# Attention and a hyper-mixer on one core: the third batch's load ahead of the output weights, later loads half a batch earlier, and x transposed in two 64-row tiles

## Chip, cores, metric

One core of a Trainium2 chip. The metric is the device time of one execution in microseconds (us). Each kernel was run several times beside the kernel before on the same chip. A profiled execution is one of them; times inside it count from its first instruction. TensorE's clock is given as a share of full speed; a "dip" is a stretch at half of it. A run is marked slow when it is over 1.5% above the fastest of the same kernel; ratios leave slow runs out.

## The reference

Eight batches. Each is grouped-query attention (16 query heads, 4 key/value heads, 384 rows, head size 64), whose output x [384, 1024] goes through a mixer and an output product:

```python
scores = scale * q @ k.T ; attn = softmax(scores) ; x = attn @ v      # per head, heads joined
wq, wk = x @ w_q, x @ w_k                                              # [384, 64] each
mixed  = (scale * wq @ wk.T) @ x
out    = relu(mixed) @ w_out                                           # [384, 1024]
```

## The kernel before

Batches are numbered from 0. One batch has 18 "scores" (pairs of matmuls, L259, for two heads in two 64-row tiles of TensorE), each followed by one exponential on ScalarE. Every three scores end in an attention step that writes a part of x (`xnat`). Two such steps complete one 128-row block of x. The first two blocks of batches 1 to 7 are transposed by DMA, the third by TensorE; then the product of x with w_q and w_k (`wqk`) reads all three. A small scheduler in the program fixes TensorE's order when the kernel is built, using guessed times such as `DMA_TR` for a DMA transpose. If a guess is wrong, TensorE waits in that order.

```python
def load(b):                       # keys, queries in two halves, values; 2.36 MB; all on the SP queue
    ...
def tr_dma(b, part):               # part 0: keys; parts 1 to 3: queries of one 128-row block
    ...
    nc.sync.dma_start_transpose(out=KT, ...)              # or QT[...]
    ready["K", b, kp] = clk["pe"] + DMA_TR                # the scheduler's guess
def attend(b, g, u):
    ...                            # attention of one group; when a block of x is whole:
    if x_by_dma(b, c) and kp == KP - 1:
        x_tr_dma(b, c)             # nc.sync.dma_start_transpose(out=xTs[b][:, :, c, :], ...)
def x_by_dma(b, c):
    return b > 0 and c < C - 1
def x_tr(b, c):                    # by TensorE: eight 128x128 transposes into one PSUM bank, one copy
    ...
def after_s(b, s):                 # after score s of batch b
    n = b + 1
    if b == 0 or n >= B: return
    if s == 0: load(n)
    elif s == 5: cast(n); start_tr(n)
    elif s in (9, 11, 13, 15): tr_dma(n, (s - 9) // 2)
# the start, cut
load(0); ...; load(1)
# w_q, w_k: two loads; then the output weights, 4.19 MB in four pieces:
for dc in range(0, DC, 2):
    nc.sync.dma_start(out=wld[:, dc:dc + 2, :], in_=moe_w_out[...])
```

Keys and queries of batches 0 and 1 are transposed by TensorE, those of later batches by DMA. Each of these DMA instructions goes to one in-order queue on SP; loads, DMA transposes and result stores share it.

The softmax here doesn't subtract the row's maximum and nothing guards it: scores larger than these inputs give would overflow.

## Time and profile before

| | before |
|---|---|
| time, us | 224.5 median (223.93 to 226.09) on the first chip |
| profiled span, us | 224.3 (an execution of 226.12) |
| TensorE, VectorE, ScalarE, GpSimd busy | 95%, 65%, 63%, 23% |
| wait on the third batch's query transpose | 2.87 us |
| mean granted clock | 0.985 |

To read it: TensorE is the bound, so what counts is where it idles or runs at half clock. The share of busy time says little; the two places are given line by line in the prediction. The profiled execution is one of the slower ones of this kernel (226.12, against 224.69 in the median of three others).

### The profile page before, as it was taken

The numbers are of one execution on the slowest core, as the hardware profiler recorded it, in microseconds if no ns is written. First come the engines' busy times: TensorE is split into PE (matmuls) and PEld (weight loads), VectorE is DVE, ScalarE is ACT, GpSimd is POOL, SyncE is SP. The second block draws the span as 40 slices with busy tenths as digits, with TensorE's granted clock in tenths as the row PEclk, the third lists the DMA queues.
The fourth block names the chain that finished last, engine by engine and source line by source line (L and its number), as shares of the span: only waits on it lengthen the run. The fifth ranks groups of instructions, "written<-read, shape, count | busy, mean of one in ns | idle before, by whom it ended". The sixth has DMA issues, their size and how long they took to land.

```text
span 224.3 us, 5470 instructions
## 1 busy us (share of the span) xinstructions
PE 214.2 (95%) x2217; PEld 113.6 (51%) x2244; DVE 145.2 (65%) x365; ACT 140.6 (63%) x146; POOL 52.1 (23%) x97
## 2 busy tenths in 40 slices
PE   8999999589999999999999999999999999999993
PEld 5666665245545545454555546554555553434441
DVE  2355786834697758865887648874679569576332
ACT  3599998747788778887887887887888600000000
POOL 1385678406300540045016100620000000000000
PEclk9999999959999999999999999999999999999999
DMA  6996999999399979999999998989224422242424
GB/s 174 324 327 170 410 386 325 136 237 323 65 183 215 335 166 187 222 338 216 223 229 342 154 213 260 281 205 154 99 91 53 143 93 93 93 190 93 180 101 187
DMA packets 71688, 46.09 MB, mean 205 GB/s; under 512 B 42736, under 2 KB 67568, under 8 KB 71664
## 3 DMA queue, kind: packets, MB, share of 16 engines
q1 hardware_dynamic: 71520, 45.62, 77.6%
q8 instruction: 17, 0.28, 0.5%
q10 hardware_dynamic: 144, 0.13, 0.2%
q14 instruction: 7, 0.06, 0.1%
HBM read 23.59 MB, written 12.58 MB: 161 GB/s over the span
## 4 chain that ended last, share of the span: by engine, by line
PE 74%; DMA 14%; DVE 3%; SPq 3%; POOL 3%; issue 1%; DVEq 0%
PE bank L408 37%; PE bank L282 13%; PE sc L259 12%; DMA qraw<-in_q_dram 12%; PE bank L331 4%; SPq L129 3%; PE bank L384 3%; PE bank L362 2%; DMA QT<-qb 2%; PE bank L322 1%; POOL qb L158 1%; DVE osb L421 1%; PE bank L349 1%; DVE msb L389 1%; POOL wqk_sb L596 1%
## 5 line engine op out<-in xcount | busy, mean ns | idle before, releaser
L263 ACT ACTIVATE pt<-sc 128x1024 bf16<-128x1024 f32 x144 | 138.9, 1023 | 34.6 <-PE sc L259 34.4
L408 PE MATMUL bank<-wout_sb,msb 128*128 128x512 bf16 x357 | 91.7, 382 | 1.3 <-issue 0.5
L408 PEld LDWEIGHTS <-msb 128*128 128x128 bf16 x384 | 33.8, 98 | 42.4 <-issue 13.7
L259 PE MATMUL sc<-QT,KT 64*128 64x512 bf16 x288 | 47.5, 387 | 3.1 <-DMA QT<-qb 2.9
L282 PEld LDWEIGHTS <-pt 128*128 128x128 bf16 x1152 | 41.9, 98 | 15.8 <-issue 9.9
L282 PE MATMUL bank<-vext,pt 128*128 128x65 bf16 x1152 | 46.9, 195 | 0.4 <-DVE osb L421 0.2
L421 DVE COPY osb<-bank 128x512 f32<-128x512 f32 (+1 forms) x49 | 33.1, 677 | 21.7 <-PE bank L408 20.5
L289 DVE TENSOR_TENSOR xnat<-bank,rcp 128x256 bf16<-128x256 f32 x96 | 40.8, 425 | 3.3
L389 DVE TENSOR_SCALAR msb<-bank 128x384 bf16<-128x384 f32 x64 | 32.5, 551 | 9.5 <-PE bank L384 9.0
L287 DVE RECIPROCAL rcp<-bank 128x4 f32<-128x4 f32 x96 | 16.9, 176 | 17.6 <-PE bank L282 16.7
L158 POOL CAST qb<-qraw 128x768 bf16<-128x768 f32 x30 | 24.0, 827 | 17.4 <-DMA qraw<-in_q_dram 15.1
L153 POOL CAST kb<-kraw 128x192 bf16<-128x192 f32 x30 | 9.2, 347 | 67.3 <-DMA kraw<-in_k_dram 67.3
L259 PEld LDWEIGHTS <-KT 64*128 64x128 bf16 x288 | 12.4, 94 | 24.1 <-issue 17.2
L117 PE MATMUL bank<-idle 128*128 128x256 bf16 x80 | 14.8, 324 | 1.0 <-DVE idle L562 1.0
L331 PE MATMUL bank<-xT,wqk_sb 128*128 128x384 bf16 x64 | 11.7, 327 | 0.0
L117 PEld LDWEIGHTS <-idle 128*128 128x128 bf16 x80 | 7.9, 114 | 6.6 <-issue 4.0
L384 PE MATMUL bank<-wT,Csb 64*128 64x384 bf16 x32 | 10.6, 332 | 0.4 <-DVE rcp L287 0.3
L384 PE MATMUL bank<-wq,Csb 64*128 64x384 bf16 x32 | 10.6, 332 | 0.0
L599 POOL CAST wout_sb<-wld 128x1024 bf16<-128x1024 f32 x8 | 8.1, 1040 | 4.1 <-DMA wld<-in_moe_w_out_dram 4.1
L366 DVE CAST Csb<-bank 128x512 bf16<-128x512 f32 x8 | 5.5, 688 | 5.2 <-PE bank L362 5.2
L337 DVE CAST wT<-bank 128x384 bf16<-128x384 f32 x8 | 4.5, 558 | 6.7 <-PE bank L331 6.7
L323 DVE COPY xT<-bank 128x1024 bf16<-128x1024 bf16 x10 | 6.9, 688 | 2.5 <-PE bank L322 2.5
(33 smaller groups left out, 70.1 us busy)
## 6 DMA issues: line engine op xcount, KB each, us to landing
out_dram<-osb SPq DMA_DIRECT2D x23, 512.0 KB, 3.1
qraw<-in_q_dram SPq DMA_DIRECT2D x15, 768.0 KB, 7.4
wld<-in_moe_w_out_dram SPq DMA_DIRECT2D x4, 1024.0 KB, 9.5
kraw<-in_k_dram SPq DMA_DIRECT2D x7, 384.0 KB, 4.3
vraw<-in_v_dram SPq DMA_DIRECT2D x7, 384.0 KB, 8.9
qraw<-in_q_dram SPq DMA_DIRECT2D x1, 512.0 KB, 5.3
kraw<-in_k_dram SPq DMA_DIRECT2D x2, 192.0 KB, 3.7
vraw<-in_v_dram SPq DMA_DIRECT2D x2, 192.0 KB, 6.3
```

What stands on the lines that cost most here:

```text
L117: nc.tensor.matmul(out=bank_ps[i][:, :256], lhsT=idle[:, :P], rhs=idle, start=True, stop=True)
L158: eng.tensor_copy(out=nats[b][1][:, :, kp, :, u, :].rearrange("p c i d -> p i c d"), in_=raws[b][2][:, h0:h0 + G])
L259: nc.tensor.matmul(out=ps[:, u, :], lhsT=KT[lo:hi, kp * C + kc, :], rhs=QT[lo:hi, t0:t0 + G, :].rearrange("k i p -> k (i p)"), start=True, ...
L263: nc.scalar.activation(out=pt.rearrange("k u i p -> k u (i p)"), in_=ps, func=AF.Exp, scale=attn_scale)
L282: nc.tensor.matmul(out=ps[:, i * DE:i * DE + D + 1], lhsT=tiles[kc][:, u, i, :], rhs=vext[:, 2 * kp + u, kc, :D + 1], start=(kc == 0), sto ...
L287: nc.vector.reciprocal(out=rcp, in_=avv[:, :, D])
L289: nc.vector.tensor_tensor(out=xnats[b][:, c, h0:h0 + G, :], in0=avv[:, :, :D], in1=rcp.to_broadcast([P, G, D]), op=ALU.mult)
L331: nc.tensor.matmul(out=ps, lhsT=wqk_sb[:, dc, :], rhs=xT[:, dc].rearrange("d c p -> d (c p)"), start=(dc == 0), stop=(dc == DC - 1))
L384: nc.tensor.matmul(out=bank_ps[i][:, :S], lhsT=Csb[lo:hi, j * P:(j + 1) * P], rhs=w[lo:hi, :], start=True, stop=True)
L389: nc.vector.tensor_scalar_max(out=msb[:, dc, :], in0=bank_ps[i][:, :S], scalar1=0.0)
L408: nc.tensor.matmul(out=ps, lhsT=msbs[b][:, dc, c * P:(c + 1) * P], rhs=wout_sb[:, dc, half * NH:(half + 1) * NH], start=(nd == 0), stop=(n ...
L421: nc.vector.tensor_copy(out=osb[:, n0:n1], in_=ps[:, n0 - half * NH:n1 - half * NH])
```

## The change

The intent: the third batch (batch 2) is needed at about 42 us, the output weights at about 46 to 50; so load batch 2 first. Later batches are then loaded half a batch earlier too. And x transposed by TensorE is done in pairs of 64-row tiles that run side by side, next to scores, which use the same tiles. The diff is cut and shortened:

```diff
         if part == 0: ...
-                ready["K", b, kp] = clk["pe"] + DMA_TR
+                ready["K", b, kp] = max(clk["pe"], 32000.0) + DMA_TR        # "Q" likewise
     def x_tr(b, c):
-        for dc in range(DC):
-            nc.tensor.transpose(out=ps[:, dc, :], in_=xn[:, c, dc*P:(dc+1)*P], identity=ident)
-        nc.vector.tensor_copy(out=xTs[b][:, :, c, :], in_=ps)
+        for dc in range(DC):
+            for half in range(2):                       # lo:hi = 64 rows
+                nc.tensor.transpose(out=outs[half][:, dc, :], in_=xn[lo:hi, c, dc*P:(dc+1)*P],
+                                    identity=ident[lo:hi, lo:hi])
+        for half in range(2):
+            nc.vector.tensor_copy(out=xTs[b][:, :, c, half*H:(half+1)*H], in_=outs[half])
     def after_s(b, s):
+        if s == 9 and 1 <= b < B - 2: load(b + 2)
-        if s == 0: load(n)
-        elif s == 5: cast(n); start_tr(n)
-        elif s in (9, 11, 13, 15): tr_dma(n, (s - 9) // 2)
+        if s == 1: (cast(n) if n > 2); start_tr(n)
+        elif n == 2 and 4 <= s < 8: tr_dma(n, s - 4)
+        elif n > 2 and s in (4, 7, 10, 13): tr_dma(n, (s - 4) // 3)
 # start: after the loads of w_q and w_k
+    load(2)                                             # before the output weights
 # and after the casts of w_q and w_k
+    cast(2)                                             # before the casts of the output weights
```

More of the change, by code (lines that the diff above doesn't have):

```diff
@@ L197, in tr_dma @@
             for kp in range(KP):
-                ready["Q", b, kp, c] = clk["pe"] + DMA_TR
+                ready["Q", b, kp, c] = max(clk["pe"], 32000.0) + DMA_TR
     def tr_k(b, kp0, kp1):
@@ L318, in x_tr @@
         xn = xnats[b].rearrange("p c h d -> p c (h d)")
-        _, i = bank()
-        ps = bank_ps[i].bitcast(BF16).rearrange("p (n t) -> p n t", n=DC)
+        two = [bank(half)[1] for half in range(2)]
+        H = P // 2
+        outs = [bank_ps[i].bitcast(BF16)[:, :DC * H].rearrange("p (n t) -> p n t", n=DC) for i in two]
         for dc in range(DC):
-            nc.tensor.transpose(out=ps[:, dc, :], in_=xn[:, c, dc * P:(dc + 1) * P], identity=ident)
-        nc.vector.tensor_copy(out=xTs[b][:, :, c, :], in_=ps)
-        ready["T", b, c] = bank_free[i] = on("dve", 690, pe(450))
+            for half in range(2):
+                lo, hi = half * H, (half + 1) * H
+                nc.tensor.transpose(out=outs[half][:, dc, :], in_=xn[lo:hi, c, dc * P:(dc + 1) * P],
+                                    identity=ident[lo:hi, lo:hi])
+        end = pe(8 * 34, "row")
+        for half in range(2):
+            nc.vector.tensor_copy(out=xTs[b][:, :, c, half * H:(half + 1) * H], in_=outs[half])
+            ready["T", b, c] = bank_free[two[half]] = on("dve", 420, end)
     def wqk(b):
@@ L433, in after_s @@
     def after_s(b, s):
+        if s == 9 and 1 <= b < B - 2:
+            load(b + 2)
         n = b + 1
-        if b == 0 or n >= B:
+        if b < 1 or n >= B:
             return
-        if s == 0:
-            load(n)
-        elif s == 5:
-            cast(n)
+        if s == 1:
+            if n > 2:
+                cast(n)
             start_tr(n)
-        elif s in (9, 11, 13, 15):
-            tr_dma(n, (s - 9) // 2)
+        elif n == 2 and 4 <= s < 8:
+            tr_dma(n, s - 4)
+        elif n > 2 and s in (4, 7, 10, 13):
+            tr_dma(n, (s - 4) // 3)
     def cand_s():
@@ L483, in chain_open @@
             if not x_by_dma(b, c):
-                todo.append((lambda c=c: when(("X", b, c, 0), ("X", b, c, 1)), lambda c=c: x_tr(b, c), 1))
+                todo.append((lambda c=c: when(("X", b, c, 0), ("X", b, c, 1)), lambda c=c: x_tr(b, c), 2, "tiled"))
         todo.append((lambda: max(when(*[("T", b, c) for c in range(C)]), ready["Wt"]), lambda: wqk(b), 1))
```

## The prediction

> **What bounds the kernel now.** I read the page's slice table first, then the list of waits, the chain that ended last, the timeline of TensorE and of the SP queue from 0 to 56 us, and last a table of windows around the one place where the slice table dips.
>
> ```profile
> PE   8999999589999999999999999999999999999993
> ACT  3599998747788778887887887887888600000000
> PEclk9999999959999999999999999999999999999999
> ```
>
> A slice is 5.6 us. TensorE is busy at 90% or more in all but a few slices; the only deep dip, and the only dip of the granted clock, is slice 8 (44.9 to 50.5 us). ScalarE is done by slice 30, so the last 50 us are TensorE alone.
>
> ```profile
> PE sc L259 <- DMA QT<-qb: 2.9, 1, 2.9
> ...
> 24.88 14.96 DMA qraw<-in_q_dram
> 39.90 1.60 POOL qb L158 x2
> 41.53 3.79 DMA QT<-qb
> ```
>
> The first line is from TensorE's waits: the one wait of weight is for the transposed queries of the third batch (batch 2). The rest is the chain: its queries were 15 us under way, were cast at 39.90, transposed by DMA from 41.53, and TensorE waited for them.
>
> ```profile
> 18.27 3.80 SPq L573 DMA_DIRECT2D wld<-in_moe_w_out_dram  x4
> 22.20 0.39 SPq L129 DMA_DIRECT2D kraw<-in_k_dram  x1
> 22.77 8.86 SPq L129 DMA_DIRECT2D qraw<-in_q_dram  x2
> 31.73 3.35 SPq L129 DMA_DIRECT2D vraw<-in_v_dram  x1
> ...
> 38.75 1.61 SPq L190 DMA_TRANSPOSE KT<-kb  x1
> 41.53 2.62 SPq L195 DMA_TRANSPOSE QT<-qb  x2
> ```
>
> The SP queue shows why. The 4 MB of output weights are queued before batch 2, whose loads land behind them. Yet the first product with the output weights runs only at 49.98 us:
>
> ```profile
> 42.03 0.39 PE L259 MATMUL sc<-QT,KT 64*128 64x512 bf16 x2
> ...
> 45.45 0.61 PE L259 MATMUL sc<-QT,KT 64*128 64x512 bf16 x2 [2.87 <-DMA QT<-qb]
> ...
> 49.98 1.52 PE L408 MATMUL bank<-wout_sb,msb 128*128 128x512 bf16 x3
> 51.44 0.61 PE L259 MATMUL sc<-QT,KT 64*128 64x512 bf16 x4
> ```
>
> ```profile
> 42.00:46.00 4.00, 1.13 (x11) 0.26 (x7) 2.01 (x7) 1.55 (x2) 0.40 (x1) 0.77 0.97 172
> 46.00:51.00 5.00, 5.00 (x39) 2.59 (x39) 2.24 (x6) 3.07 (x3) 0.22 (x1) 0.50 0.98 241
> 51.00:56.00 5.00, 4.92 (x55) 2.54 (x54) 2.41 (x6) 3.52 (x4) 3.11 (x7) 1.00 1.08 323
> ```
>
> Columns are window, length, busy time with count of PE, PEld, DVE, ACT, POOL, then clock, DMA share, GB/s. The 2.87 us wait pulls the clock to half (the trace has the drop at 44.15 and the return at 50.98), so the 39 matmuls of 46 to 51 us run at half speed. That is the second, larger-looking part of the price. Until about 42 us scores come at ScalarE's pace (dummy matmuls fill TensorE); from 51 us on TensorE's work alone sets the end: in each 24 us window from 56 to 176 us it lacks only 0.2 to 0.7 us.
>
> **What the Trainium skill says.** (1) "TensorE: Matmul & The Clock Gate", part 1: the gate passes half or all pulses, decided over free-running windows of 3413 ns. The trace agrees: 50.98 - 44.15 = 6.83 us, two such windows. The first of the windows held TensorE work until 42.57, so even a half idle window was enough here. (2) "DMA: Bandwidth & Descriptors", section on queues, rings and completion order: each engine takes one queue's descriptors in ring order. All loads and transposes here are on one queue, and landings follow issue order: value loads at 41.0, an x transpose at 43.2 to 43.4, keys at 44.4, queries at 45.3. (3) "TensorEngine Tiling (Array Packing)", key properties: tiles run in parallel, but a change of tiling mode drains TensorE. Trace: two score pairs take 0.54 us to the next matmul (34.53 to 35.07), one pair 0.32 (36.10 to 36.42); so a pair is 0.22 and a mode change 0.10 us.
>
> **The change, part by part.**
>
> *Loads.* Batch 2 moves ahead of the output weights; later batches are loaded half a batch earlier. No byte is added. The trace has 768-byte loads at about 328 GB/s and the weights at about 410 GB/s. The weights' first packets come at about 21.5 us; put batch 2 (2.36 MB) there and it takes 7.2 us, so its last queries land at about 27.5 to 29 and are cast by about 30 (0.8 us per cast). The transposes can then be issued at about 27 (keys) and 30 us (queries), instead of 38.75 and 41.53. But they are on the same queue behind the weights (4.19 MB, 10.2 us), which end where batch 2 ended before: about 39 us on most DMA engines. On the straggling engines a landing comes about 1.4 us later (the weights' fourth piece: 32.55 and 34.01), so 40.4. The transposes move together in the trace: while one engine is late the others stop. Then keys and first queries, 768 and 1024 packets of 256 bytes at about 1,100 packets per us (1,057 in the 1.25 us after 40.5 with a slow start, 1,140 per us from 44.25), need 1.6 us less what was done early, and 0.5 to 1 us to the semaphore. This gives 42 to 43.5 us, against a need at about 42.5. A 16 KB instruction fetch stops all transposes from 41.75 to 43.0 in the trace before; it comes with TensorE's instruction count, and 48 more rows before it move it ahead some 1.5 us, into the weights' tail. I take a remaining wait of 0.6 us. Gain here 2.87 - 0.6 = 2.3 us.
>
> *Clock.* From the first score of batch 2 (45.45) to its fourth (51.44) TensorE took 5.99 us. At full clock the same row is: three score pairs with their two mode changes 3 x 0.32 = 0.96, five dummies 0.55, a relu-mix pair with change 0.27, 24 attention matmuls with change 0.85, four output matmuls with change 0.97, together 3.6 us. Gain 2.4 us if the clock holds. With 0.6 us of idle in a window instead of about 1.6 I give this three in four: 1.8 us expected.
>
> *Output weights.* Their casts end about 42.4 us (fourth piece 40.4, two casts of 1.0 us). First use, without the stall, is about 45.6. This should cost nothing.
>
> *x transposes.* Eight 128-row transposes take 8 x 0.056 = 0.45 us and one mode change:
>
> ```profile
> 28.14 0.62 PE L322 MATMUL bank<-ident,xnat 128*128 128x128 bf16 x8
> 28.69 0.39 PE L259 MATMUL sc<-QT,KT 64*128 64x512 bf16 x2
> ```
>
> Sixteen half tiles in pairs of 64 columns: a score pair starts 3 ns apart in the trace, and 65-column attention matmuls follow each other at 31 ns, so a pair is about 31 to 34 ns and eight pairs 0.27. Saved 0.18 us, times seven batches on TensorE's path = 1.3 us; batch 0 lies in the ScalarE-paced part and gets dummies instead (80 before, 82 after). Against it stands the order of instructions as built: from the first score of batch 2 on, mode changes go from 140 to 153, because five more relu-mix pairs and two x transposes stand alone between full-array work. 13 x 0.10 = 1.3 us. Net zero. VectorE copies two halves (420 ns each by the 128x512 row) for one of 688: 10 x 0.15 us, on an engine 72 to 75% busy there; nothing.
>
> Sum: 2.3 + 1.8 + 0 = 4.1, or 220.6 us. That is a mean; the likeliest single course is that the wait vanishes (5.3, see below), so I place the prediction between the two, at a gain of 4.7: 224.7 - 4.7 = 220.0 us. This placing is my choice.
>
> **The rivals.** *The wait vanishes.* For it: batch 2's data are ready 10 us earlier and the transposes are queued in time. Then 2.87 + 2.4 = 5.3, 219.4 us, or 218.5 if the tiled transposes give something net. *The wait only moves.* The transposes land behind the weights at 43.5 to 44, TensorE idles 1 to 1.5 us; for it speak ring order and the equal sum of bytes. With the clock held 220.6, with the clock dropped again about 223. *A new wait.* In later batches two query transposes and the second x transpose now queue behind an early load (7 us); the x transpose has some 9 scores, about 10 us, before its use, so little margin; with the weights' cast late as well, 224 to 226. Against it: SP's ring has been as full before without a wait after 51 us. *Slack eats the gain:* a later idle stretch on TensorE swallows what is saved. Against it: there is next to none after 51 us.
>
> **Range and chances.** Faster by over 2% means under 220.2. I give the vanished wait 0.4, the moved wait with clock held 0.25 (half of it just under the line), moved with clock dropped 0.3, new wait 0.05. So faster 0.52, within 2% 0.44, slower 0.04; range 217.8 to 223.4.
>
> **What would show it.** Right: issue of the key and query transposes of batch 2 near 27 to 33 us; first score of batch 2 near 42.5 to 43; clock whole in slice 8; first output matmul near 46; no wait for the output weights' cast; the distance from the fourth score of batch 2 to the end unchanged within 0.5 us; x transposes in about 0.27 us. Wrong: a wait of over 1 us on the query transpose, a second clock dip, waits of the x-to-query-and-key product for a DMA in batches 2 to 6, or tiled transposes that take 0.45 us or more.

## The result

| | before | changed |
|---|---|---|
| time, us (first chip) | 224.5 (223.93 to 226.09, 4 runs) | 231.42 (230.02 to 232.1, 4 runs) |
| ratio | | 1.0288 [1.0217, 1.036] |
| profiled span, us | 224.3 | 229.8 |
| first score of batch 2, us | 45.45 | 43.32 |
| fourth score of batch 2, us | 51.44 | 46.93 |
| from there to the end, us | 172.9 | 182.9 |

A ratio is the mean time of one kernel's fast runs over that of the other's of the same rounds, so it is not quite the ratio of the medians quoted.

It is slower by 2.9%; I had predicted 220.0 and a range of 217.8 to 223.4. The table's last three rows already place the loss: up to the fourth score of batch 2 the change gains 4.5 us, and after it loses 10.0.

The slice table of the changed kernel (a slice is 5.7 us; slices are counted from 0):

```profile
PE   8999999841999999999999999999999999999993
ACT  2499999950388778787788678768878750000000
PEclk9999999995699999999999999999999999999999
```

Before, TensorE dipped to 5 tenths in slice 7 and the clock in slice 8. Now there is a hole in slices 8 and 9, with TensorE at 4 and 1 and ScalarE at 5 and 0, and the clock dip follows in slices 9 and 10. TensorE's waits in the changed kernel name it (us in total, times, longest):

```profile
PE bank L338 <- DMA xT<-xnat: 8.1, 2, 7.9
...
PE sc L259 <- DMA QT<-qb: 0.9, 1, 0.9
```

The wait that the change was to remove is down from 2.9 to 0.9 us. A new one of 7.9 us stands ahead of L338, the product of x with w_q and w_k: it waits for a DMA transpose of x. The timeline of TensorE in the changed kernel shows whose:

```profile
43.32 0.39 PE L259 MATMUL sc<-QT,KT 64*128 64x512 bf16 x2 [0.93 <-DMA QT<-qb]
...
45.97 1.03 PE L415 MATMUL bank<-wout_sb,msb 128*128 128x512 bf16 x3
46.93 0.60 PE L259 MATMUL sc<-QT,KT 64*128 64x512 bf16 x4
47.37 0.40 PE L326 MATMUL bank<-ident,xnat 64*128 64x64 bf16 x16
...
56.73 2.72 PE L338 MATMUL bank<-xT,wqk_sb 128*128 128x384 bf16 x8 [7.89 <-DMA xT<-xnat]
59.38 1.04 PE L259 MATMUL sc<-QT,KT 64*128 64x512 bf16 x4
```

Batch 2 starts as hoped, at full clock: the scores take 0.39, not the 0.61 of before, and the output product is met at 45.97 without a wait. Then x of batch 1 is transposed by TensorE (its third block) and the product must wait, because one of its DMA blocks is not there. It then runs at half clock: eight matmuls take 2.72 us. The SP queue of the changed kernel shows why the block is late:

```profile
27.16 6.57 SPq L190 DMA_TRANSPOSE KT<-kb  x1
33.84 9.02 SPq L195 DMA_TRANSPOSE QT<-qb  x3
42.96 1.25 SPq L313 DMA_TRANSPOSE xT<-xnat  x1
44.26 0.58 SPq L129 DMA_DIRECT2D kraw<-in_k_dram  x1
44.89 1.16 SPq L129 DMA_DIRECT2D qraw<-in_q_dram  x2
46.09 2.19 SPq L129 DMA_DIRECT2D vraw<-in_v_dram  x1
48.39 3.32 SPq L313 DMA_TRANSPOSE xT<-xnat  x1
```

I read the duration of a line as including the time for which the queue is too full to take it: one x transpose took 1.25 us, the keys' transpose behind the weights 6.57. The last of the batch 2 transposes was taken at 42.86, behind the weights, so everything after them is late. Then comes the fourth batch's load, in the middle between the two x transposes of batch 1. The second of them, whose block of x was complete at 40.0, is issued at 48.39; TensorE wants it from 48.83, and it lands only at 56.6, behind 2.36 MB:

```profile
48.39 8.20 DMA xT<-xnat
```

(This is from the chain of work that ended last in the changed kernel: start, duration, what.)

### The profile page after: what moved, and what is told of

Same layout as the page of the kernel before. It is cut to its first block, busy times and chain, and to the rows that moved or that the text cites. A ratio compares the mean times of both kernels' runs of the same rounds, so it can differ in the third digit from the quotient of the medians.

```text
span 229.8 us, 5645 instructions
## 1 busy us (share of the span) xinstructions
PE 212.8 (93%) x2298; PEld 111.0 (48%) x2326; DVE 146.0 (64%) x375; ACT 140.4 (61%) x146; POOL 52.1 (23%) x97
## 4 chain that ended last, share of the span: by engine, by line
PE 71%; DMA 19%; SPq 4%; issue 2%; DVE 1%; POOL 1%; DVEq 0%
PE bank L415 36%; PE bank L282 12%; PE sc L259 12%; DMA xT<-xnat 6%; DMA qraw<-in_q_dram 5%; PE bank L338 5%; DMA wld<-in_moe_w_out_dram 4%; DMA QT<-qb 4%; SPq L129 3%; PE bank L391 3%; PE bank L369 2%; DVE wT L344 1%; PE bank L356 1%; PE bank L326 1%; POOL qb L158 1%
## 5 line engine op out<-in xcount | busy, mean ns | idle before, releaser
L415 PEld LDWEIGHTS <-msb 128*128 128x128 bf16 x384 | 32.9, 98 | 45.0 <-issue 17.8
L259 PE MATMUL sc<-QT,KT 64*128 64x512 bf16 x288 | 47.0, 385 | 1.2 <-DMA QT<-qb 0.9
L282 PEld LDWEIGHTS <-pt 128*128 128x128 bf16 x1152 | 41.1, 97 | 14.1 <-issue 6.7
L282 PE MATMUL bank<-vext,pt 128*128 128x65 bf16 x1152 | 46.2, 193 | 0.1
L338 PE MATMUL bank<-xT,wqk_sb 128*128 128x384 bf16 x64 | 13.0, 350 | 8.1 <-DMA xT<-xnat 8.1
L338 PEld LDWEIGHTS <-wqk_sb 128*128 128x128 bf16 x64 | 6.1, 102 | 12.6 <-issue 9.2
L330 DVE COPY xT<-bank 128x512 bf16<-128x512 bf16 x20 | 7.5, 418 | 4.6 <-PE bank L326 4.4
```

The lines of the kernel that those rows point to most:

```text
L259: nc.tensor.matmul(out=ps[:, u, :], lhsT=KT[lo:hi, kp * C + kc, :], rhs=QT[lo:hi, t0:t0 + G, :].rearrange("k i p -> k (i p)"), start=True, ...
L282: nc.tensor.matmul(out=ps[:, i * DE:i * DE + D + 1], lhsT=tiles[kc][:, u, i, :], rhs=vext[:, 2 * kp + u, kc, :D + 1], start=(kc == 0), sto ...
L338: nc.tensor.matmul(out=ps, lhsT=wqk_sb[:, dc, :], rhs=xT[:, dc].rearrange("d c p -> d (c p)"), start=(dc == 0), stop=(dc == DC - 1))
L415: nc.tensor.matmul(out=ps, lhsT=msbs[b][:, dc, c * P:(c + 1) * P], rhs=wout_sb[:, dc, half * NH:(half + 1) * NH], start=(nd == 0), stop=(n ...
```

## The experiments

**Theory A**: the load of the fourth batch (batch 3), issued ahead of the second x transpose of batch 1, makes that transpose late; all the loss comes from this. **Rival B**: the DMA engines are full there in any case. **Rival C**: the tiled transposes do it. A second question is what the two halves of the change are worth without the accident.

All results first. Each row is compared with runs of the kernel before on the same chip: rows 1 to 4 with the same 7 runs on the second chip (median 222.46), rows 5 to 8 with these and one more (222.36), rows 9 to 11 with 11 runs on the third (222.85). The ratios use fast runs alone:

| run | us, median | ratio to before | what TensorE waited for in its profile |
|---|---|---|---|
| late_load | 222.0 | 0.998 [0.988, 1.009] | queries 0.6 |
| loads_only | 228.5 | 1.027 [1.018, 1.035] | x 5.6, queries 1.0 (listed under ScalarE) |
| x_tiles_only | 223.2 | 1.001 [0.992, 1.011] | queries 2.1 |
| load3_pool_queue | 234.75 (two fast runs: 232.2) | 1.042 [1.030, 1.054] | x 9.3 and 0.6, queries 0.5 |
| late_load_full_x | 221.6 | 0.995 [0.988, 1.001] | queries 0.7 |
| late_load_b1 | 225.2 | 1.010 [1.003, 1.017] | x 3.1 in batch 2 and 0.9 in batch 4, queries 0.8 |
| split_wout | 222.0 | 0.994 [0.985, 1.002] | x 2.1, weight cast 0.4 |
| x1_on_pe | 220.9 | 0.992 [0.986, 0.998] | queries 1.6 |
| before_load3_early | 229.1 | 1.026 [1.019, 1.032] | x 4.5, queries 1.1 |
| changed_again | 231.2 | 1.035 [1.029, 1.042] | x 8.2 and 1.0, queries 1.6 |
| x1_pe_split | 221.2 | 0.991 [0.987, 0.995] | weight cast 0.6 |

At the line of 2%, load3_pool_queue and changed_again are slower, loads_only and before_load3_early are unclear (their intervals begin just under 1.02, but well above 1), and all others count as the same.

### 1. The loads behind the x transposes

```diff
-        if s == 9 and 1 <= b < B - 2:
+        if s == 17 and 1 <= b < B - 2:
             load(b + 2)
```

> The early loads (fourth batch on) are issued at score 17 of a batch instead of score 9, so behind the second x transpose of the same batch, not ahead of it; TensorE's instruction order is the same as in the changed kernel. Theory A (the x transpose of batch 1 lay in ring order behind the fourth batch's 2.36 MB): the 7.9 us wait and the clock dip after it go; 7.9 + 0.3 + about 2.3 us less than the changed kernel's 231.4, so about 220 to 221.5 us. Rival B (the DMA engines are simply full there, whatever the order): the wait stays at 4 us or more, 225 us or more. Rival C (the tiled x transposes or the query transposes slow things by themselves): no change, 230 or more.

TensorE's instruction order is identical to the changed kernel's; only the place of four loads per batch in the SP queue differs. Median 222.0; in the two executions near full clock 220.43 and 221.06, in the two at clock 0.992 222.94 and 223.35. Where those two dip isn't known, as the profiled one is at 0.998. Windows around the hole in the changed kernel (window, length, busy time with count of PE, PEld, DVE, ACT, POOL, then clock, DMA share, GB/s):

```profile
48.50:56.50 8.00, 0.33 (x11) 0.21 (x7) 1.08 (x5) 0.85 (x1) 4.86 (x9) 0.67 1.18 254
56.50:61.50 5.00, 4.58 (x17) 1.78 (x19) 1.30 (x3) 1.42 (x2) 0.00 (x0) 0.51 0.00 0
```

and the same windows with late loads:

```profile
48.50:56.50 8.00, 8.00 (x90) 3.98 (x88) 5.78 (x16) 5.96 (x7) 4.68 (x9) 1.00 1.18 270
56.50:61.50 5.00, 5.00 (x49) 2.20 (x48) 4.46 (x13) 4.05 (x5) 0.64 (x2) 1.00 1.20 158
```

The hole and the dip are gone, and the two executions near full clock lie in the 220 to 221.5 that theory A gave; the median does not. The DMA engines move as many bytes in the first window as in the changed kernel (270 against 254 GB/s), so being busy is not what hurts: the order is. Theory A holds here; C falls, and so does B in the form that the engines are full whatever the order. From the fourth score of batch 2 (46.42) to the end (218.65) it now takes 172.2 us instead of 182.9.

### 2. The same loads with the old x transposes

x_tr and its place in the list as before, the rest as changed.

> The changed kernel with the x transposes as before (eight full 128-row transposes in one bank); loads as changed. Theory A: the wait for the x transpose of batch 1 stays (TensorE's use of it is one score pair later, so about 7 us instead of 7.9), 229.5 to 231.5 us. Rival C (the tiled transposes cause the loss): back to about 220 to 224 us.

228.5 us, a wait of 5.6 us for x, clock 0.985 in the profile:

```profile
PE bank L331 <- DMA xT<-xnat: 5.6, 1, 5.6
```

So the tiles are not needed for the loss, and C falls again. The wait is shorter than the 7 us I expected and the time a little under my 229.5.

### 3. The tiled x transposes alone

The kernel before, with only `x_tr` and its list entry from the change.

> The kernel before with the tiled x transposes alone. My working says seven times 0.2 us saved against 13 more mode changes of 0.1 us: 224.5 us within 0.7. Rival: the tiles are worth what the author hoped, 1.3 to 1.8 us: 222.9 or less. Rival C: they cost several us: 228 or more.

1.001 with an interval of 1% either side: no effect that the times can show. The profiles can: from the fourth score of batch 2 to the end before takes 172.89 us and this kernel 172.23. The pair late_load_full_x and late_load says the same, 172.91 and 172.23. So in two pairs of single profiles the tiles net 0.7 us, not zero.

### 4. The fourth batch's load on another DMA queue

```diff
-            load(b + 2)
+            load(b + 2, nc.gpsimd if b == 1 else None)     # the DMAs of this one load issued by GpSimd
```

> The changed kernel with the fourth batch's load issued at the same place but from GpSimd, so on another DMA queue; all else the same. Theory A (order within one ring): the second x transpose of batch 1 no longer lies behind 2.36 MB and lands 3 to 5 us after its issue; the wait of 7.9 us falls below 3 us; 221 to 226 us. Rival B (the bytes themselves): the transpose shares the engines with the load and the wait stays above 5 us, 228 us or more.

This was to tell ring order from bytes, and A in the narrow form I had written (order within one ring, that is, one queue's list of work) failed: 234.75 us in the median, a wait of 9.3 us. That is what rival B of this expectation, the bytes themselves, had forecast (over 5 us, 228 or more). Both x transposes of batch 1 were now issued in time, at 42.44 and about 43.8:

```profile
42.44 3.60 SPq L314 DMA_TRANSPOSE xT<-xnat  x2
```

but landed 8.3 to 13.7 us later. Here are TensorE's wait and, from the view of the x transposes' line between 40 and 62 us, the time to landing, in this run:

```profile
PE bank L339 <- DMA xT<-xnat: 9.8, 2, 9.3
...
DMA to landing us min/median/max: 8.3/11.0/13.7
```

The packets in the trace show how. From 49 to 53 us there are 275 of the transposes' 256-byte packets beside 202 of 4608 bytes of the load, between one and two for each; from 45.5 to 46.5, where the trace has no packet of 4608 bytes, 955 of the transposes' pass in one us. This fits what the Trainium skill, "DMA: Bandwidth & Descriptors", section on queues, rings and completion order, says: an engine takes turns between queues packet by packet. A packet there is a group of descriptors, which need not be what the trace records as one, so this is a fit and not a proof. As I read it, a transpose cut into small packets that takes turns with large ones gets a small part of the engine. So theory A needs its wider form: the load must not be in flight **ahead of or beside** the x transpose.

Two things keep this from being a clean test of order against bytes. GpSimd did not have to wait for SP's full queue, so the load was issued at 41.74, ahead of both x transposes and 2.5 us earlier than in the changed kernel. And its packets were 4608 bytes, where SP's loads have 768. A queue that keeps the small packets was not tried, so "another queue does not help" is shown for GpSimd's alone.

### 5. Both halves set right, old transposes

Late loads as in 1, x_tr as before.

> The changed kernel with both suspects set right: early loads at score 17 and x transposes as before (eight full ones). What is left of the change is batch 2 ahead of the output weights. If the tiled x transposes net to nothing (1.3 us of transposes against 1.3 us of mode changes), this equals the run with late loads and tiles within 0.7 us on the same clock, that is 220 to 221.5 us in executions without a clock dip. If the tiles are worth 1.3 us or more, this is 222 us or more; if they cost that, 219.5 or less. Against the kernel before on the same chip: 1.5 to 2.5 us faster in executions without a dip.

221.6 us, all six runs at full clock or 0.998: just above the expectation of 220 to 221.5, which three of the six runs exceed. This kernel is what is left of the loads' idea: batch 2 ahead of the weights. Against the full-clock runs of before on that chip (221.89 to 222.51) it gains about 0.6 us, less than the 1.5 to 2.5 I expected. The queries' wait is 0.7 us; the 2.9 of before is from a dipped execution, and the point on the clock below shows that it need not be that long.

### 6. Only the fourth batch's load behind

```diff
-        if s == 9 and 1 <= b < B - 2:
+        if s == (17 if b == 1 else 9) and 1 <= b < B - 2:
```

> As the run with late loads, but only the fourth batch's load (issued in batch 1) is put at score 17; the loads of batches 4 to 7 stay at score 9. Theory: only batch 1 was hurt, because only there the queue was so late that the x transpose of the second block fell behind the load. Then the same as late loads, about 220.5 us without a dip, and no wait of the x-to-query-and-key product. Rival: later batches' x transposes are delayed too and the late loads helped there: 1 us or more slower than late loads.

My theory said that batch 1 alone was hurt, and it fell: batch 2 now waits for its own x transpose, with its own clock dip (0.992), and the time is 225.2. Batch 4 waits too, for 0.9 us: the list names VectorE, but the x transpose landed at 121.07 and the product started at 121.12. TensorE's timeline:

```profile
73.97 1.63 PE L338 MATMUL bank<-xT,wqk_sb 128*128 128x384 bf16 x8 [3.06 <-DMA xT<-xnat]
```

In the changed kernel the long wait in batch 1 may have given the queue time to catch up, and so hidden this second one; no run tests that. So the load at score 9 also hurts a later batch, once batch 1 no longer waits.

### 7. Half of the output weights behind the transposes

On top of 1, the second half of the weights and its casts moved to behind the third batch's last query transpose:

```diff
-    for dc in range(0, DC, 2):              # in the start: only the first half stays
+    for dc in range(0, DC // 2, 2):
 ...
             tr_dma(n, s - 4)
+            if s == 7: load and cast weight rows DC // 2 to DC
```

> Late loads, and the second half of the output weights (2 MB and its casts) put behind the third batch's transposes. Theory: the wait of 0.6 to 0.9 us left before batch 2's first score is these transposes lying behind 4 MB of weights; with 2 MB of it behind them, they land at about 36 to 38 us and the wait goes. So TensorE starts batch 2 at about 42.4 us, and the second dip cause is gone: about 0.7 us less than late loads without a dip, 219.5 to 220.5, unless the first output product at about 46 us now waits for the cast of weight rows 4 and 5; then up to 2 us more.

The first score of batch 2 starts at 41.93 us with no wait for queries, as expected; the wait moves again: 2.1 us for batch 1's x transposes, now behind the 2 MB of weights, and 0.4 us for a cast. So other bytes ahead of the x transposes, here the weights', make them late too. 222.0 us: no gain over 1, where 219.5 to 220.5 was hoped for.

### 8. Batch 1's x blocks transposed by TensorE

```diff
     def x_by_dma(b, c):
-        return b > 0 and c < C - 1
+        return b > 1 and c < C - 1
```

> The changed kernel with its early loads, but batch 1's first two x blocks are transposed by TensorE (32 more half tiles, VectorE copies) and not by DMA. If the whole loss came from that one DMA transpose of batch 1, the loss goes although the load stays at score 9: about 221 to 222 us (two x transposes of 0.3 us more than late loads), and no wait of the x-to-query-and-key product. If the early load hurts by other ways (contention, casts, later batches): 225 us or more.

The early loads stay at score 9, and the loss is gone: 220.9 us, 0.992 of before [0.986, 0.998], with no wait for x in any batch. The one DMA wait left on TensorE's list is

```profile
PE sc L259 <- DMA QT<-qb: 1.6, 1, 1.6
```

Taking batch 1's two DMA-transposed blocks off the queue, of which one lay behind the load, removes some 10 us. This and 1 take away the two sides of the same pair, and agree.

### 9. The load put early in the kernel before

```diff
-        if s == 0:
+        if s == 0 and n != 3:
             load(n)
 ...
             tr_dma(n, (s - 9) // 2)
+            if b == 1 and s == 13: load(3)
```

> The kernel before with one thing changed: the fourth batch's load is issued some six scores earlier, just ahead of the second x transpose of batch 1 (TensorE's order is unchanged). If a load ahead of that transpose is enough to make the loss, without any other part of the change: the transpose (used at 54.7 us in the profile of before) lands at about 57 us, so a wait of 2 to 3 us on it appears, and one or two half clock windows with it: 225 to 229 us. If the loss needs the rest of the change: 222 to 225 us and no such wait.

Moving one batch's load (four DMAs) five scores ahead, with the same TensorE order, makes the kernel before 2.6% slower. SP queue and TensorE:

```profile
43.23 0.57 SPq L129 DMA_DIRECT2D kraw<-in_k_dram  x1
43.84 1.15 SPq L129 DMA_DIRECT2D qraw<-in_q_dram  x2
45.04 1.91 SPq L129 DMA_DIRECT2D vraw<-in_v_dram  x1
47.05 4.16 SPq L313 DMA_TRANSPOSE xT<-xnat  x1
```

```profile
55.49 2.74 PE L331 MATMUL bank<-xT,wqk_sb 128*128 128x384 bf16 x8 [4.52 <-DMA xT<-xnat]
```

The pattern of the changed kernel, made by that move alone (the wait is 4.5 us, more than the 2 to 3 I expected). So in this kernel a load ahead of the transpose is enough for the loss (9), and with the load behind it (1) or that transpose gone (8) the loss is gone too.

### 10. The changed kernel again

> The changed kernel itself, on the chip of this call, as a control: 1.02 to 1.04 times the kernel before, wait of 7 to 8 us for the x transpose of batch 1 in the profile.

1.035 on the third chip, with the same wait (8.2 us, just over the 7 to 8 expected): the result is not one chip's.

### 11. A version better than both

Experiment 8 with the split weights of 7.

> A candidate for the best: batch 1's x blocks transposed by TensorE, loads as in the changed kernel, and the second half of the output weights (with its casts) behind the third batch's transposes. The wait of 1.6 us on the query transpose goes (first score of batch 2 at about 41.9 us) and there is no x transpose to wait for in batch 1; 1.0 us less than the run with batch 1's x on TensorE: about 219.5 to 220 us, if the first output products don't wait over 0.5 us for the weights' cast. Otherwise equal to that run, 220.5 to 221.

221.2 us, 0.991 [0.987, 0.995], every run at clock 0.997 or more. The first score of batch 2 is at 42.23 us without a wait, but the first output product waits for the cast of weight row 5:

```profile
46.38 0.38 PE L415 MATMUL bank<-wout_sb,msb 128*128 128x512 bf16 x1 [0.61 <-POOL wout_sb L458]
```

so it is equal to experiment 8 within the noise, not a us better. Both beat the kernel before by some 0.8 to 0.9%, which counts as the same at the line of 2%. Some of that is that the kernel before dips more often: mean against mean of the runs at clock 0.997 or more it is 0.6 to 0.7%.

## Why the prediction was wrong, point by point

- **The bound and the wait to be removed: right.** Keys of batch 2 were issued at 27.16 (predicted about 27), queries at 33.84 (about 30; the full queue held the keys' issue for 6.57 us). The first score came at 43.32 (42.5 to 43), with 0.9 us of wait left (0.6). The instruction fetch that I thought would move ahead by 1.5 us, out of the transposes' way, moved from 41.25 to 40.82 only (there are 18 such fetches for the changed kernel's 4624 matmuls and weight loads, 17 for the 4461 of before), and fewer than 10 of the transposes' packets per quarter us pass from 41.5 to 42.5. Two readings of the slices were off by one and change nothing: TensorE dips in slice 7, only the clock in slice 8, and ScalarE works until slice 31, so TensorE is alone for some 45 us, not 50.
- **The output weights: right.** First product at 45.97 (about 46), no wait.
- **The clock there: right for the changed kernel, over-sized as a gain.** The clock held over the start of batch 2: from the first to the fourth score it took 3.61 us, against 3.6 predicted. But I took the dip of the profiled execution as a property of the kernel before. Of its 19 runs on the second and third chip 13 ran at clock 0.999 or 1.000 and took 221.6 to 223.0 us; only six dipped (clock 0.985 to 0.992, 224.0 to 225.9 us). The term of 1.8 us was there to be had in about a third of the executions. The term of 2.3 us for the wait comes from the same execution of 226.12, though both were taken off the median of 224.7. Experiment 9's kernel runs the same instructions as before up to its moved load, and in its profile batch 2 starts so:

```profile
43.94 0.39 PE L259 MATMUL sc<-QT,KT 64*128 64x512 bf16 x2 [1.15 <-DMA QT<-qb]
...
47.56 0.60 PE L259 MATMUL sc<-QT,KT 64*128 64x512 bf16 x4
```

The wait is 1.15 us, without a dip; the queries' transposes were issued at 39.87 there, and at 41.53 in the profile of before. The changed kernel's fourth score, at 46.93, is 0.6 us ahead of this one, not 4.5. So much of the predicted gain was the price of that one execution; how often it is paid on the first chip isn't recorded. My rule that half an idle window is enough for a dip (the window before the drop, 40.74 to 44.15) does not hold either: a gap of 2.06 us dipped in experiment 3, and one of the same length in experiment 7 did not.
- **x transposes: nearly right.** Sixteen half tiles and a mode change took 0.33 us in the changed kernel (47.37 to 47.70), so eight pairs 0.23, against 0.27 predicted. The net was 0.7 us, not zero.
- **The step that failed: the rival "a new wait".** The prediction said: "the x transpose has some 9 scores, about 10 us, before its use, so little margin", and then "Against it: SP's ring has been as full before without a wait after 51 us", and gave it 0.05. Two errors lie in it. I looked at "later batches" and, in the list of what would prove me wrong, at batches 2 to 6; the victim was batch 1. The load is issued between the two x transposes of batch 1, and the built order of the SP queue shows that before any run. And I counted the margin in scores from a queue that runs on time, though my own working for batch 2 had this queue stuck behind the weights until about 40 us: the x transpose, its block complete at 40.0 us, was issued at 48.39 and took 8.2 us instead of 3.4. The size too was wrong: a wait of 7.9 us plus the half clock after it, and not the 4 to 6 us that 224 to 226 us stood for.
- **The ledger.** Profile to profile the end moved by 229.8 - 224.3 = +5.5 us. Up to the fourth score of batch 2: -4.5. After it +10.0, of which the wait is 7.9, half clock from 56.73 to 61.44 (half of 4.7) 2.4, the tiles -0.7, and 0.4 is left over in small waits. The medians differ by more, 6.9 us: the profiled execution of before was one with a dip, and slower than its median. Against the undipped start of experiment 9's profile the first term would be -0.6.

What stays open: why some executions dip and others don't (experiment 1 dips in two of four with a wait of 0.6 us in the profile of another). That experiment 5 gains about 1 us less than expected fits a wait of some 1.15 us in the undipped executions of before (1.15 - 0.74 = 0.4, against 0.6 measured); no profile of such an execution exists, so it isn't shown.

## What to carry to other kernels

When a transfer is moved ahead in a queue, list what now lies behind it and when each of those is used; the first victim here was the small transfer that used to slip in just in time, and it paid for all bytes ahead of it. The one second queue that was tried was no way out. And a forecast sized on a single profile should first be held against the spread of the runs. Take a clock dip, too, as something that some executions have: look at the clock of all runs before its removal is counted as gain.

## What the Trainium skill lacked or had wrong

- "DMA: Bandwidth & Descriptors", queues, rings and completion order: it says that engines take turns between queues packet by packet, but not what this does to a DMA transpose. Here one of 256 KB landed 3.3 to 3.4 us after its issue when no load lay before it, 8.2 us behind a 2.36 MB load in the same queue, and 13.7 us beside that load in GpSimd's queue.
- The same page: it does not say that a transpose nearly stops while the loads ahead of it have not ended on every engine. In the trace of before, between 39.5 and 40.5 us only 48 of the transposes' packets pass, beside 58 of 768 bytes of the loads, and 797 from 41.0 to 41.75. That the late engines hold up the others is read off, not tested; the trace views don't tell the engines apart.
- No page has this: after a 16 KB instruction fetch DMA transposes nearly stop. In before it starts at 41.25, and from 41.75 to 43.0 only 36 of their packets pass. The same hole follows the fetch at 40.82 in the changed kernel (24 packets from 41.5 to 42.5) and at 40.43 in experiment 1 (32 from 41.0 to 42.25). This is read off too.
- "TensorE: Matmul & The Clock Gate", part 1 and the summary table: it has the half clock follow a whole idle window and warns of gaps over about 3 us. Here idle gaps of 2.87 us (before) and 2.06 us (experiment 3) dipped, the drop coming 1.6 us into the gap in both; a gap of 2.06 us in experiment 7 did not dip, nor did 1.6 us (experiment 8) and less, in the profiles. The dips' lengths fit its window of 3413 ns: 3.41 us in experiments 6 and 9, 6.83 us before, 10.24 us (three windows) in the changed kernel.
- "TensorEngine Tiling (Array Packing)", key properties: it says that a change of mode drains TensorE, without a cost. Here it is 0.10 us (one score pair to the next full matmul 0.32 us, a pair 0.22).
